# Cosine attention, FFT mixing and MLP on one core: identity-matmul transposes for the first two batches, three weight chunks in flight, five row buffers

## The chip, the cores and the metric

The kernel runs on one core of a Trainium2 chip. The core has a matrix engine (TensorE; PE in the profile, with PEld for the loading of its stationary operand), a vector engine (VectorE, DVE), a scalar engine (ScalarE, ACT), GpSimd (POOL), SyncE (SP), and 16 DMA engines that serve the queues of SP and POOL. SBUF is the on-chip memory of 128 partitions; PSUM has 8 banks of 512 f32 values per partition and takes what TensorE computes. The metric is the device time of one execution in microseconds, the median of several runs.

## What is computed

```python
q_n = q / (norm(q, axis=-1) + 1e-06)          # q, k, v: [8, 12, 448, 64]
k_n = k / (norm(k, axis=-1) + 1e-06)
attn = softmax(q_n @ k_n.T / tau)             # tau = 0.1
x = (attn @ v), heads side by side            # [8, 448, 768]
u = x + real(fft(fft(x, axis=1), axis=2))
un = (u - mean(u)) / sqrt(var(u) + 1e-06)     # over the 768
out = u + maximum(un @ w_ch1, 0) @ w_ch2      # 768 -> 3072 -> 768
```

## The kernel before

The eight batches run one after another through the same stages, and stages of neighbouring batches overlap. A planner in Python (class `Plan`) takes every operation with its possible engines, a modelled duration, a priority and the names that it reads and writes; `schedule()` builds one static list per engine from that, and `emit()` writes each list with semaphore waits. At run time each engine goes through its list in order: an instruction that waits holds everything behind it on its engine. PSUM is shared out as three pools of tiles: M has two tiles (one bank each; the outputs of the MLP matmuls), G two (two banks each; scores and FFT), V one (two banks; PV).

*Rows of Q and K.* A batch has seven row blocks: three of Q and three of K with 128 rows, and a tail block with the last 64 rows of each. `norm(b)` loads a block (SP), squares it (ScalarE, L584), sums each head (VectorE, L586), takes logarithm and exponential for the norm (ScalarE, `norms`, L463 and L465), and scales the rows to bf16 (VectorE, L592) into a buffer QH. Of QH's four rows of 768, two take scaled rows from batch 2 on and the other two serve as an f32 buffer for the squares; batch 1 uses all four for scaled rows. A DMA transpose on SP then writes QT (or KT): 64 channels of two heads on the partitions, tokens along the row. Batch 0 is handled by `first_norm`, in two groups of six heads: K and Q with the tail are scaled, and four DMA transposes (L545) write KT and QT. Copies into KTD place the 64 tail tokens of K for two heads on a block diagonal.

*Scores.* The FFT over tokens is folded: token s and token 448 - s are handled together. So the scores of two heads are computed in two halves of 225 columns, first tokens 0 to 224 read from QT, then token 0 followed by tokens 447 down to 224 read from QR, a copy of QT in reversed order (`qdup` and `qrev`; VectorE and ScalarE for batch 0, POOL at L627 after). QK is at L674, with the tail at L686 and L687. ScalarE takes the exponential (L655), PV follows (L702 for the tail of V in VZ, L705), then reciprocal, scaling, fold and the FFT matmuls (`fft`, L752 and L785).

*Normalized rows.* Each block of u is normalized by VectorE (L842) and transposed by DMA on SP (L846) into unT, inside the buffer UNT.

*MLP.* `ffn(b)` computes h = W1 x unT in 24 groups of six matmuls (L874), evacuated with relu by ScalarE or VectorE (L883, L884), and y = hT x W2 in groups of 24 (L895), added to u (L904) and stored. The MLP of batch 0 goes in two passes, first one block of rows (128 columns), then two (256 columns); the others have 384 or 512 columns. TensorE's list mixes the MLP of one batch with the attention of the next.

*Weights.* `weights` brings W1 and W2 in 12 chunks each, cast to bf16 by DMA from POOL's queue; each waits until the second last before it has landed. Loads of batch 2 on SP are gated on the tenth chunk of W2 (`self.w[21]`), loads of batch 1 on the scaled rows of batch 0 (`raw0`) and one transpose (`trs[3]`), the first loads of V on a transpose of batch 0.

## Time and profile before

| | us |
|---|---|
| median of 3 runs (677.9 to 682.45) | 677.96 |
| the profiled execution, whole | 682.08 |
| its span in the trace | 679.9 |
| TensorE busy | 594.6 (87%) |
| VectorE busy | 379.3 (56%) |
| ScalarE busy | 337.3 (50%) |
| GpSimd busy | 99.4 (15%) |

A busy time is the union of the instructions of one engine; the modelled ends of TensorE's matmuls overlap. "PEclk" is the TensorE clock that was granted, as a share of full speed. An idle time carries the releaser that the trace infers: what ended last before the instruction began. L12 is line 12 of the kernel. A line in the group view can hold several shapes ("+3 forms"), and then its mean is a mean over them.

### The profile page before, as it was taken

How to read it: one execution, taken by the hardware profiler on the slowest of the kernel's cores; microseconds unless marked ns; L12 is line 12 of the kernel's file. 1: busy time of each engine (PE TensorE's matmuls, PEld its weight loads, DVE VectorE, ACT ScalarE, POOL GpSimd, SP SyncE). 2: the span in 40 equal slices, each digit the busy share in tenths (PEclk: the TensorE clock that was granted, in tenths of full speed). 3: DMA queues.
4: the chain of work that ended last, by engine and by line, in shares of the span. 5: the costliest groups of instructions: out<-in, count | busy, mean ns of one | idle time of the engine just before them, and what ended most of it. 6: DMA issues, size and time to landing. Idle time of an engine off the chain costs nothing.

```text
span 679.9 us, 12298 instructions
## 1 busy us (share of the span) xinstructions
PE 594.6 (87%) x5040; PEld 372.0 (55%) x5040; DVE 379.3 (56%) x808; ACT 337.3 (50%) x608; POOL 99.4 (15%) x127
## 2 busy tenths in 40 slices
PE   0364578996999879998999999989999999999996
PEld 0143456763456546674556566755565667654463
DVE  5658723595575776559655964586758233810010
ACT  7686346622675138724674358534763256404300
POOL 2612242300100410021002110211020010000001
PEclk9988578997999989999999999999999999999998
DMA  8999999998734935095419561957157310210011
GB/s 179 125 181 144 139 176 132 168 125 180 109 60 80 138 90 108 20 131 137 93 37 118 107 156 34 113 92 163 25 67 72 78 48 1 44 50 24 0 47 48
DMA packets 210264, 65.29 MB, mean 96 GB/s; under 512 B 194080, under 2 KB 207904, under 8 KB 210208
## 3 DMA queue, kind: packets, MB, share of 16 engines
q1 hardware_dynamic: 152288, 41.70, 35.3%
q0 software_dynamic: 57920, 22.81, 27.0%
q8 instruction: 40, 0.66, 0.4%
q14 instruction: 16, 0.13, 0.1%
HBM read 51.90 MB, written 11.01 MB: 93 GB/s over the span
## 4 chain that ended last, share of the span: by engine, by line
PE 55%; DMA 4%; DVE 1%; issue 1%; POOL 1%; POOLq 0%; SPq 0%; DVEq 0%
PE PS L895 23%; PE PS L874 22%; PE PS L674 3%; DMA QT<-QH 3%; PE PS L705 3%; PE PS L752 1%; PE PS L702 1%; PE PS L785 1%; DVE QH L592 1%; POOL QR L627 1%; PE PS L687 0%; PE PS L686 0%; DMA UNT<-F 0%; POOLq L956 0%; DVE AC L734 0%
## 5 line engine op out<-in xcount | busy, mean ns | idle before, releaser
L874 PE MATMUL PS<-UNT,W1b 128*128 128x512 bf16 (+3 forms) x1296 | 245.6, 344 | 31.3 <-DMA UNT<-F 20.9
L895 PE MATMUL PS<-W2b,hT 128*128 128x384 bf16 x1344 | 226.6, 328 | 0.0
L874 PEld LDWEIGHTS PS<-UNT,W1b 128*128 128x128 bf16 x1296 | 122.4, 102 | 128.3 <-issue 30.9
L655 ACT ACTIVATE E<-PS 128x900 bf16<-128x900 f32 (+1 forms) x192 | 149.0, 825 | 87.0 <-PE PS L674 80.4
L895 PEld LDWEIGHTS PS<-W2b,hT 128*128 128x128 bf16 x1344 | 130.7, 98 | 86.3 <-issue 4.3
L883 ACT ACTIVATE hT<-PS 128x512 bf16<-128x512 f32 (+3 forms) x139 | 69.2, 498 | 100.9 <-PE PS L874 93.2
L904 DVE TENSOR_TENSOR OUTB<-PS,U 128x384 f32<-128x384 f32 x56 | 31.0, 554 | 107.4 <-PE PS L895 107.1
L884 DVE TENSOR_SCALAR hT<-PS 128x512 bf16<-128x512 f32 (+3 forms) x77 | 44.6, 579 | 64.3 <-PE PS L874 64.0
L674 PE MATMUL PS<-QT,KT 64*128 64x225 bf16 x288 | 35.4, 270 | 35.7 <-DVE QR L929 25.5
L592 DVE TENSOR_TENSOR QH<-STG,RN 128x768 bf16<-128x768 f32 x42 | 40.0, 953 | 27.6 <-DMA QT<-QH 15.6
L919 POOL DMA_INDIRECT out_dram<-OUTB,IDX x20 | 20.4, 1019 | 232.7 <-DVE OUTB L904 154.9
L705 PE MATMUL PS<-VB,E 128*128 128x65 bf16 x1152 | 53.5, 196 | 0.0
L635 POOL DMA_DIRECT2D VB<-in_v_dram x24 | 25.2, 1054 | 190.2 <-PE PS L705 185.3
L705 PEld LDWEIGHTS PS<-VB,E 128*128 128x128 bf16 x1152 | 50.1, 100 | 2.4
L702 PE MATMUL PS<-VZ,E 128*128 128x130 bf16 x192 | 43.1, 224 | 4.7 <-DMA VZ<-in_v_dram 2.9
L586 DVE TENSOR_REDUCE SS<-QH 128x12 f32<-128x768 f32 x42 | 39.4, 938 | 9.2 <-ACT QH L584 9.1
L674 PEld LDWEIGHTS PS<-QT,KT 64*128 64x128 bf16 x288 | 14.3, 94 | 52.9 <-DVE QR L929 25.5
L806 DVE TENSOR_TENSOR U<-SQT,X 128x384 bf16<-128x384 f32 (+3 forms) x80 | 42.3, 570 | 0.7
L584 ACT ACTIVATE QH<-STG 128x768 f32<-128x768 f32 x42 | 35.3, 840 | 10.1 <-DMA STG<-in_k_dram 9.4
L717 DVE RECIPROCAL RD<-PS 128x8 f32<-128x8 f32 x48 | 9.8, 204 | 52.5 <-PE PS L705 52.1
L674 PE MATMUL PS<-QR,KT 64*128 64x225 bf16 x288 | 35.0, 267 | 0.0
L719 DVE TENSOR_TENSOR X<-PS,RD 128x512 bf16<-128x512 f32 x48 | 33.1, 690 | 1.3
(92 smaller groups left out, 467.8 us busy)
## 6 DMA issues: line engine op xcount, KB each, us to landing
STG<-in_q_dram SPq DMA_DIRECT2D x18, 384.0 KB, 4.4
STG<-in_k_dram SPq DMA_DIRECT2D x18, 384.0 KB, 5.2
VB<-in_v_dram POOLq DMA_DIRECT2D x24, 192.0 KB, 7.2
W1b<-in_moe_w_ch_dram POOLq DMA_DIRECT2D x12, 384.0 KB, 6.2
W2b<-in_moe_w_ch_dram POOLq DMA_DIRECT2D x12, 384.0 KB, 6.0
out_dram<-OUTB SPq DMA_DIRECT2D x8, 384.0 KB, 2.5
hT<-in_q_dram SPq DMA_DIRECT2D x7, 192.0 KB, 5.6
hT<-in_k_dram SPq DMA_DIRECT2D x2, 576.0 KB, 5.0
```

The source lines that it names most:

```text
L584: P.add("act", lambda a, sq=sq, buf=buf: a.activation(sq, buf, ACTF.Square), t_act(DM), pr, f"sq{i}_{b}", reads=bn, writes=sqn, margin=1.0)
L586: P.add("dve", lambda v, i=i, sq=sq: v.tensor_reduce(SS[:, i, :], v3(sq), AX.X, AluOp.add), t_dve(DM), pr, f"ss{i}_{b}", reads=sqn, writes ...
L592: P.add("dve", lambda v, i=i, buf=buf, qh=qh: v.tensor_tensor(v3(qh), v3(buf), RN[:, i, :].unsqueeze(2).to_broadcast((128, H, DH)), AluOp. ...
L655: return a.activation(o, self.PS[:, bk:bk + nc_, 0:SQ2], ACTF.Exp, scale=1.0 / self.tau)
L674: i = pe.matmul(self.PS[:, bk + h, c0:c0 + NK], self.KT[r, jj, kt * 128:(kt + 1) * 128], Q[r, jj, 0:NK], start=True, stop=True)
L702: pe.matmul(o, st(6), self.VZ[:, j, :], start=True, stop=False, skip_group_check=True)
L705: r = pe.matmul(o[:, 65 * h:65 * h + 65], st(2 * kt + h), self.VB[:, kt, 2 * j + h, :], start=False, stop=(h == 1 and kt == 2), skip_group ...
L806: return v.tensor_tensor(U[o0:o0 + n, ut, cs].rearrange("p (i e) -> p i e", e=2), src, X[i0:i0 + n, x, cs].rearrange("p (i e) -> p i e", e ...
L874: r = pe.matmul(self.PS[:, bk, 0:n], self.W1b[:, j, ft * 128:(ft + 1) * 128], unT[:, j, cs], start=(j == 0), stop=(j == NJ - 1))
L883: return e.activation(self.hT[:, ft, cs], self.PS[:, bk, 0:n], ACTF.Relu)
L884: return e.tensor_relu(self.hT[:, ft, cs], self.PS[:, bk, 0:n])
L895: r = pe.matmul(self.PS[:, bk, 0:384], self.hT[:, ft, 128 * i:128 * i + 128], self.W2b[:, ft, 384 * c:384 * c + 384], start=(ft == 0), sto ...
```

## The change

1. The ScalarE program starts with an explicit load of the table set `natural_log_exp_and_others`.
2. VectorE builds ID, a 128 x 128 identity in bf16.
3. Batch 0: scaled K, Q and tail go through matmuls with ID as the moving operand into M tiles (three, five and three matmuls: `tk`, `tq`, `tt`), evacuated by ScalarE or VectorE into KT, QT and KTD, in place of four DMA transposes. The tail of Q and K is written to a place of its own. Column 448 of QT gets a second copy of token 0.
4. Batch 1: each scaled row block goes through two tiles of three identity matmuls (`tp`) with an evacuation each, in place of a DMA transpose; KTD is filled from the tail's matmuls.
5. Normalized rows of batch 0: six identity matmuls in the V tile (`tn`) and two evacuations, in place of a DMA transpose, three times.
6. QR is gone. QK reads QT backwards, columns 448 down to 224; from batch 1 on POOL copies the one column 448.
7. QH has five rows: four take scaled rows in every batch, the fifth takes squares in two halves of 384 from batch 2 on.
8. A weight chunk waits for the third last before it, not the second last.
9. Gates: the first three loads of batch 1 wait for the scaled rows of the first head group alone and are ordered after a load of batch 0 in place of a transpose; the first V loads wait for a load of batch 0 in place of a transpose.

```diff
+                if e == "act":
+                    nc.scalar.preload_act_table_set("natural_log_exp_and_others")
...
-        self.QH = T("QH", [128, 4, DM])
+        self.QH = T("QH", [128, 5, DM])
         self.QT = T("QT", [128, NJ, 512])
-        self.QR = T("QR", [128, NJ, NK])
...
+        P.add("dve", lambda v: v.tensor_scalar(self.ID[:], kcf[:, 0:128], self.rowf[:, 0:1], None, AluOp.is_equal), 0.3, -3, "id",
+              reads=["OUT1", "rowf"], writes=["ID"])
...
-        prev = [start, start]
+        prev = [start, start, start]
...
-            prev.append(P.add("pool", fn, 1.0, 9, nm, writes=[nm], dma=(nm, 16), after=[prev[-2]], serve=2.1))
-        self.w = prev[2:]
+            prev.append(P.add("pool", fn, 1.0, 9, nm, writes=[nm], dma=(nm, 16), after=[prev[-3]], serve=2.1))
+        self.w = prev[3:]
...
-                              ("Q", Q, [f"Sq{t}{g}" for t in range(3)], 18, uf[:, 0:1536], ["QL"]),
-                              ("T", R, [f"St{g}"], 6, uf[:, 0:1536], ["QLt"])], sq))
+                              ("Q", Q, [f"Sq{t}{g}" for t in range(3)], 18, uf[:, 0:1152], ["QL"]),
+                              ("T", R, [f"St{g}"], 6, uf[:, 1152:1536], ["QLt"])], sq))
...
-                if i == 1:
-                    continue
-                if i == 0:
-                    dst, src, rd, wr = self.KT[:, 3 * g:3 * g + 3], qh, qhn, [f"KT{t}_{g}" for t in range(3)]
-                else:
-                    dst, src, rd, wr = self.QT[:, 3 * g:3 * g + 3], qh, ["QL", "QLt"], [f"QT{t}_{g}" for t in range(4)]
-                dst = dst.rearrange("p j (t c) -> p (j t) c", c=128)
-                self.trs.append(P.add("sp", lambda sy, sem, dst=dst, src=src: sy.dma_start_transpose(dst, src).then_inc(sem, 16),
-                                      2.0, pr + g, f"tr{nm}{g}_0", reads=rd, writes=wr, dma=(f"t0{g}{i}", 16), serve=1.5 + 0.3 * i))
...
+            def evac(tile, dst, n, nm, wr):
+                def ev(e):
+                    i = self.PS[:, self.bank(tile), 0:n]
+                    return e.activation(dst, i, ACTF.Copy) if e is self.nc.scalar else e.tensor_copy(dst, i)
+                self.evac(ev, n, pr + g, nm, writes=wr, after=(tile.users[0],), tiles=(tile,))
+            for j in range(3):
+                jj = 3 * g + j
+                tile = Tile("M")
+
+                def fn(pe, tile=tile, j=j, kh=kh):
+                    for t in range(3):
+                        r = pe.matmul(self.PS[:, self.bank(tile), 128 * t:128 * t + 128], kh[:, 384 * j + 128 * t:384 * j + 128 * t + 128], ID[:],
+                                      start=True, stop=True)
+                    return r
+                P.add("pe", fn, 0.3, pr + g, f"tk{jj}_0", reads=kn + ["ID"], tiles=(tile,), acquire=tile)
+                evac(tile, self.KT[:, jj, :], 384, f"ek{jj}_0", [f"KT{t}_{jj}" for t in range(3)])
+                tile = Tile("M")
+
+                def fn(pe, tile=tile, j=j, qh=qh, th=th):
+                    o = self.PS[:, self.bank(tile), :]
+                    q3 = qh.rearrange("p (t c) -> p t c", t=3)[:, :, 128 * j:128 * j + 128]
+                    for t in range(3):
+                        pe.matmul(o[:, 128 * t:128 * t + 128], q3[:, t], ID[:], start=True, stop=True)
+                    pe.matmul(o[:, 384:448], th[:, 128 * j:128 * j + 128], ID[:, 0:64], start=True, stop=True)
+                    return pe.matmul(o[:, 448:449], q3[:, 0], ID[:, 0:1], start=True, stop=True)
+                P.add("pe", fn, 0.35, pr + g, f"tq{jj}_0", reads=qn + tn + ["ID"], tiles=(tile,), acquire=tile)
+                evac(tile, self.QT[:, jj, 0:449], 449, f"eq{jj}_0", [f"QT{t}_{jj}" for t in range(4)] + [f"QTd_{jj}"])
+            self.tails(pr + g, g, th, tn, 0)
...
+    def tails(self, pr, g, th, tn, b):
+
+        tile = Tile("M")
+
+        def fn(pe):
+            for j in range(3):
+                r = pe.matmul(self.PS[:, self.bank(tile), 64 * j:64 * j + 64], th[:, 128 * j:128 * j + 128], self.ID[:, 64:128],
+                              start=True, stop=True)
+            return r
+        self.P.add("pe", fn, 0.15, pr, f"tt{g}_{b}", reads=tn + ["ID"], tiles=(tile,), acquire=tile)
+        for x in range(2):
+            rows = slice(64 * x, 64 * x + 64)
+
+            def ev(e, rows=rows, x=x):
+                i = self.PS[rows, self.bank(tile), 0:192].rearrange("p (j c) -> p j c", j=3)
+                o = self.KTD[rows, 3 * g:3 * g + 3, 64 * x:64 * x + 64]
+                return e.activation(o, i, ACTF.Copy) if e is self.nc.scalar else e.tensor_copy(o, i)
+            self.evac(ev, 192, pr, f"et{g}_{b}", writes=[f"KTD{x}_{3 * g + y}" for y in range(3)], after=(tile.users[0],), tiles=(tile,))
...
-        order = [self.trs[3]] if b == 1 else []
+        order = [self.loads[9]] if b == 1 else []
...
-                after = self.raw0
+                after = self.raw0[0:3] if i < 3 else self.raw0
...
-                sqn, sq, nq = ["QH2", "QH3"], self.QH[:, 2:4, :].rearrange("p a b -> p (a b)").bitcast(F32), 2
-            P.add("act", lambda a, sq=sq, buf=buf: a.activation(sq, buf, ACTF.Square),
-                  t_act(DM), pr, f"sq{i}_{b}", reads=bn, writes=sqn, margin=1.0)
-            P.add("dve", lambda v, i=i, sq=sq: v.tensor_reduce(SS[:, i, :], v3(sq), AX.X, AluOp.add),
-                  t_dve(DM), pr, f"ss{i}_{b}", reads=sqn, writes=[f"SS{par}_{i}"])
-            self.norms(b, pr, 12 * i, 12 * i + 12, [f"SS{par}_{i}"], [f"RN{par}_{i}"])
-            r = self.qh_next % nq
+                sqn, sq, ns = ["QH4"], self.QH[:, 4, :].bitcast(F32), 2
+            w = DM // ns
+            for x in range(ns):
+                P.add("act", lambda a, sq=sq, src=buf[:, w * x:w * x + w]: a.activation(sq, src, ACTF.Square),
+                      t_act(w), pr, f"sq{i}_{b}", reads=bn, writes=sqn, margin=1.0)
+                P.add("dve", lambda v, o=SS[:, i, H // ns * x:H // ns * (x + 1)], sq=sq: v.tensor_reduce(
+                    o, sq.rearrange("p (h d) -> p h d", d=DH), AX.X, AluOp.add),
+                    t_dve(w), pr, f"ss{i}_{b}", reads=sqn, writes=[f"SS{par}_{i}" + "xy"[x]])
+            self.norms(b, pr, 12 * i, 12 * i + 12, [f"SS{par}_{i}" + x for x in "xy"[:ns]], [f"RN{par}_{i}"])
...
+            r = self.qh_next % 4
...
+            if b == 1:
+                if kind == "t":
+                    for g in range(2):
+                        self.tails(pr, g, qh[:, 384 * g:384 * g + 384], [f"QH{r}"], b)
+                for g in range(2):
+                    tile = Tile("M")
+                    n = 64 if kind == "t" else 128
+
+                    def fn(pe, tile=tile, g=g, qh=qh, n=n):
+                        for j in range(3):
+                            i = pe.matmul(self.PS[:, self.bank(tile), n * j:n * j + n], qh[:, 384 * g + 128 * j:384 * g + 128 * j + 128],
+                                          self.ID[:, 0:n], start=True, stop=True)
+                        return i
+                    P.add("pe", fn, 3 * t_mm(n), pr, f"tp{i}{g}_{b}", reads=[f"QH{r}", "ID"], tiles=(tile,), acquire=tile)
+                    dst = (self.KT if kind == "k" else self.QT)[:, 3 * g:3 * g + 3, 128 * t:128 * t + n]
+
+                    def ev(e, tile=tile, dst=dst, n=n):
+                        i = self.PS[:, self.bank(tile), 0:3 * n].rearrange("p (j c) -> p j c", j=3)
+                        return e.activation(dst, i, ACTF.Copy) if e is self.nc.scalar else e.tensor_copy(dst, i)
+                    self.evac(ev, 3 * n, pr, f"ep{i}{g}_{b}", writes=[("KT" if kind == "k" else "QT") + f"{t}_{3 * g + y}" for y in range(3)],
+                              after=(tile.users[0],), tiles=(tile,))
+                continue
...
-            for c0, c1, src, rd, nm, wr in ((0, 1, self.QT[:, :, 0:1], (0,), "qdup", "QD"),
-                                            (1, NK, self.QT[:, :, S - 1:NK - 2:-1], (1, 2, 3), "qrev", "QR")):
-                kw = dict(reads=[f"QT{t}_{y}" for y in g for t in rd], writes=[f"{wr}_{y}" for y in g])
-                if b == 0:
-                    self.copy(vw(self.QR[:, :, c0:c1]), vw(src), (c1 - c0) * n, 1, pr + g[0], f"{nm}{b}", **kw)
-                else:
-                    P.add("pool", lambda p, o=vw(self.QR[:, :, c0:c1]), i=vw(src): p.tensor_copy(o, i), t_pool((c1 - c0) * n),
-                          pr, f"{nm}{b}", **kw)
+                self.copy(self.KTD[rows, :, 64 * x:64 * x + 64], self.QT[rows, :, 448:512], 384, 4, pr, f"ktd{b}",
+                          reads=[f"QTd_{y}" for y in range(NJ)], writes=[f"KTD{x}_{y}" for y in range(NJ)])
+        if b:
+            P.add("pool", lambda p: p.tensor_copy(self.QT[:, :, 448:449], self.QT[:, :, 0:1]), 0.3, pr, f"qdup{b}",
+                  reads=[f"QT0_{y}" for y in range(NJ)], writes=[f"QTd_{y}" for y in range(NJ)])
...
-            gate = [self.trs[0 if t < 1 else 1]] if b == 0 else []
+            gate = [self.loads[8]] if b == 0 else []
...
-                        for c0, Q in ((0, self.QT), (NK, self.QR)):
+                        for c0, cols in ((0, slice(0, NK)), (NK, slice(S, NK - 2, -1))):
                             for h in (0, 1):
                                 r = slice(64 * h, 64 * h + 64)
                                 i = pe.matmul(self.PS[:, bk + h, c0:c0 + NK], self.KT[r, jj, kt * 128:(kt + 1) * 128],
-                                              Q[r, jj, 0:NK], start=True, stop=True)
+                                              self.QT[r, jj, cols], start=True, stop=True)
...
-                return pe.matmul(self.PS[:, bk, NK:SQ2], self.KTD[:, j, :], self.QR[:, j, :],
+                return pe.matmul(self.PS[:, bk, NK:SQ2], self.KTD[:, j, :], self.QT[:, j, S:NK - 2:-1],
...
+            if b == 0:
+                tile = Tile("V")
+
+                def fn(pe, tile=tile, nb_=nb_):
+                    for j in range(NJ):
+                        r = pe.matmul(self.PS[:, self.bank(tile) + j // 3, 128 * (j % 3):128 * (j % 3) + 128],
+                                      self.UN[:, nb_, 128 * j:128 * j + 128], self.ID[:], start=True, stop=True)
+                    return r
+                P.add("pe", fn, 0.4, lp, f"tn{ui}_{b}", reads=[f"UN{nb_}", "ID"], tiles=(tile,), acquire=tile)
+                for g in range(2):
+                    def ev(e, tile=tile, g=g, col=col):
+                        i = self.PS[:, self.bank(tile) + g, 0:384].rearrange("p (j c) -> p j c", j=3)
+                        o = self.unT[0][:, 3 * g:3 * g + 3, col:col + 128]
+                        return e.activation(o, i, ACTF.Copy) if e is self.nc.scalar else e.tensor_copy(o, i)
+                    self.evac(ev, 384, lp, f"eu{ui}{g}_{b}", writes=[f"unT0_{ui}" + "xy"[g]], after=(tile.users[0],), tiles=(tile,))
+                continue
```

TensorE's list at the start of the program, before (QT and QR are the two orders of Q, KTD the tail of K):

```order
L674 MATMUL PS<-QT,KT 128x225 x2
L674 MATMUL PS<-QR,KT 128x225 x2
L674 MATMUL PS<-QT,KT 128x225 x2
L674 MATMUL PS<-QR,KT 128x225 x2
L674 MATMUL PS<-QT,KT 128x225 x2
L674 MATMUL PS<-QR,KT 128x225 x2
L686 MATMUL PS<-QT,KTD 128x225
L687 MATMUL PS<-QR,KTD 128x225
```

and of the change, in the same place (QH holds the scaled K there, UNT the scaled Q and tail):

```order
L555 MATMUL PS<-ID,QH 128x128 x9
L566 MATMUL PS<-ID,UNT 128x128 x3
L567 MATMUL PS<-ID,UNT 128x64
L568 MATMUL PS<-ID,UNT 128x1
L566 MATMUL PS<-ID,UNT 128x128 x3
L567 MATMUL PS<-ID,UNT 128x64
L568 MATMUL PS<-ID,UNT 128x1
L566 MATMUL PS<-ID,UNT 128x128 x3
L567 MATMUL PS<-ID,UNT 128x64
L568 MATMUL PS<-ID,UNT 128x1
L737 MATMUL PS<-QT,KT 128x225 x4
L579 MATMUL PS<-ID,UNT 128x64 x3
```

Three K tiles and three Q tiles of the first head group now stand ahead of the first scores; the tail's tile stands behind the first four of them.

TensorE's list around the first MLP matmuls, where the FFT of batch 0 ends (L785, L848), before:

```order
L785 MATMUL PS<-CSd,Tt 128x192
L874 MATMUL PS<-UNT,W1b 128x128 x144
L874 MATMUL PS<-UNT,W1b 128x256 x30
L674 MATMUL PS<-QT,KT 128x225 x2
L674 MATMUL PS<-QR,KT 128x225 x2
```

and of the change (L652 are batch 1's Q and K, L914 the normalized rows F of batch 0, L957 the MLP's first product):

```order
L848 MATMUL PS<-CSd,Tt 128x192
L652 MATMUL PS<-ID,QH 128x64 x6
L914 MATMUL PS<-ID,F 128x128 x6
L957 MATMUL PS<-UNT,W1b 128x128 x30
L914 MATMUL PS<-ID,F 128x128 x12
L652 MATMUL PS<-ID,QH 128x128 x6
L957 MATMUL PS<-UNT,W1b 128x128 x18
L652 MATMUL PS<-ID,QH 128x128 x6
L957 MATMUL PS<-UNT,W1b 128x128 x18
L652 MATMUL PS<-ID,QH 128x128 x6
```

The pattern of the last rows goes on; 108 MLP matmuls of 128 columns stand ahead of batch 1's first scores, where 144 of 128 and 30 of 256 columns did.

ScalarE's list in the attention of batch 1 (L655 and L718 are the exponentials), before:

```order
L655 ACTIVATE E<-PS 128x900 x2
L762 ACTIVATE Tt<-PS 128x2x450
L655 ACTIVATE E<-PS 128x900
L883 ACTIVATE hT<-PS 128x256
L655 ACTIVATE E<-PS 128x450
L762 ACTIVATE Tt<-PS 128x2x450
L584 ACTIVATE QH<-STG 128x768
```

and of the change:

```order
L718 ACTIVATE E<-PS 128x900 x3
L718 ACTIVATE E<-PS 128x450
L966 ACTIVATE hT<-PS 128x256
L718 ACTIVATE E<-PS 128x900 x3
L630 ACTIVATE QH<-STG 128x384
L718 ACTIVATE E<-PS 128x450
L966 ACTIVATE hT<-PS 128x256
L718 ACTIVATE E<-PS 128x900 x3
```

The first square of a row of batch 2 (from STG) stood behind the last exponential of batch 1, beside the FFT evacuations of L762; now the first of its halves stands between the exponentials.

## Rows read from the trace of the kernel before

**Rows 1.** Windows by stage: start:end, length, busy us by engine, PEclk, DMA share, GB/s

```profile
25.50:62.20 36.70, 24.89 (x300) 16.34 (x300) 22.47 (x48) 29.43 (x41) 11.10 (x10) 0.91 1.22 170
62.20:73.60 11.40, 0.01 (x1) 0.04 (x2) 9.66 (x23) 2.41 (x7) 2.58 (x4) 0.63 1.18 126
73.60:99.00 25.40, 18.06 (x176) 15.54 (x178) 13.07 (x31) 10.49 (x35) 10.47 (x14) 0.70 1.54 162
...
130.20:163.80 33.60, 26.54 (x179) 16.72 (x177) 27.94 (x62) 10.43 (x28) 6.73 (x8) 0.95 1.06 151
163.80:600.00 436.20, 422.90 (x3602) 261.00 (x3603) 270.28 (x574) 228.73 (x413) 47.12 (x49) 0.98 0.54 87
```

**Rows 2.** Waits of PE, whole run: waiter and releaser: us, times, longest us

```profile
PE PS L674 <- DVE QR L929: 25.5, 1, 25.5
PE PS L874 <- DMA UNT<-F: 20.9, 3, 11.4
PE PS L874 <- ACT hT L883: 6.4, 4, 2.4
...
PE PS L674 <- POOL QR L627: 3.1, 2, 1.8
...
PE PS L702 <- DMA VZ<-in_v_dram: 2.9, 1, 2.9
PE PS L674 <- issue: 2.8, 2, 2.6
```

**Rows 3.** Timeline of the start: start us, us, instruction, [idle before, releaser]

```profile
12.43 1.28 ACT L463 ACT_TABLE_LOAD   x1
...
15.61 0.18 DVE L466 TENSOR_SCALAR SS<-SS 128x24 f32<-128x24 f32 x1 [2.17 <-ACT SS L465]
...
18.25 1.42 SPq L545 DMA_TRANSPOSE QT<-UNT  x1
...
25.02 0.40 DVE L929 COPY QR<-QT 128x672 bf16<-128x672 bf16 x1
```

**Rows 4.** Groups by form, from 160 us on: busy us, mean ns, idle before

```profile
L884 DVE TENSOR_SCALAR hT<-PS 128x384 bf16<-128x384 f32 x24 | 13.3, 555 | 16.0 <-PE PS L874 16.0
L883 ACT ACTIVATE hT<-PS 128x384 bf16<-128x384 f32 x48 | 23.5, 490 | 21.6 <-PE PS L874 21.4
```

**Rows 5.** Timeline, batch 0's last row transpose and first MLP matmul

```profile
67.02 11.17 SPq L846 DMA_TRANSPOSE UNT<-F  x3
...
73.59 3.36 PE L874 MATMUL PS<-UNT,W1b 128*128 128x128 bf16 x30 [11.44 <-DMA UNT<-F]
```

**Rows 6.** Timeline, batch 0's second MLP product to batch 1's first

```profile
135.65 0.96 PE L752 MATMUL PS<-CSs,F 128*128 128x225 bf16 x8 [1.42 <-DVE F L737]
...
140.43 17.71 PE L895 MATMUL PS<-W2b,hT 128*128 128x384 bf16 x108
...
158.65 0.47 DVE L842 TENSOR_SCALAR F<-U,MV,RS 128x768 bf16<-128x768 bf16 x1
...
163.78 18.83 PE L874 MATMUL PS<-UNT,W1b 128*128 128x512 bf16 x78 [5.64 <-DMA UNT<-F]
```

**Rows 7.** DMA queues, 20 to 31 us: packets, MB, share of the engines

```profile
q0 software_dynamic: 5456, 0.69, 99.4%
```

**Rows 8.** Timeline, the last rows of batch 1, from 87 to 99 us

```profile
87.31 0.96 DVE L592 TENSOR_TENSOR QH<-hT,RN 128x768 bf16<-128x768 f32 x1 [0.99 <-DMA QT<-QH]
...
97.42 1.38 POOL L627 COPY QR<-QT 128x1344 bf16<-128x1344 bf16 x1
...
98.95 0.27 PE L674 MATMUL PS<-QT,KT 64*128 64x225 bf16 x2
```

**Rows 9.** DMA, 46 to 57 us: rate in 40 slices, and the weights' queue

```profile
GB/s 0 0 0 13 73 73 97 151 192 188 188 194 184 183 184 190 201 195 199 196 123 35 71 45 32 104 181 188 192 201 194 199 147 125 162 171 190 195 199 190
...
q0 software_dynamic: 3050, 1.54, 111.3%
```

**Rows 10.** The page's groups: sums and squares of a row

```profile
L586 DVE TENSOR_REDUCE SS<-QH 128x12 f32<-128x768 f32 x42 | 39.4, 938 | 9.2 <-ACT QH L584 9.1
...
L584 ACT ACTIVATE QH<-STG 128x768 f32<-128x768 f32 x42 | 35.3, 840 | 10.1 <-DMA STG<-in_k_dram 9.4
```

57 lines of the change are left out of this document (29 added, 28 removed).

## The prediction

> **What bounds the kernel now.** I read the stages first. From 163.8 to 600 us TensorE is busy 422.9 of 436.2 us at clock 0.98 [rows 1]; there only TensorE's own work counts, and the change removes none of it. The idle time lies ahead of that. TensorE does nothing before the first scores at 25.5 us; it is busy 24.9 of 36.7 us in the attention of batch 0, not at all from 62.2 to 73.6, 18.1 of 25.4 us at clock 0.70 up to 99, and 26.5 of 33.6 us from 130 to 164 [rows 1, 5]. The waits of TensorE say for what [rows 2]: 25.5 us for the reversed copy QR of batch 0 at the start, 20.9 us in three waits for the DMA transposes of the normalized rows (UNT), 6.4 us for evacuations of hT, 2.9 us for the V tail of batch 1 (VZ), and 3.1 + 2.8 us, both at QK, where the QR copy on POOL was late (after the longest, 2.6 us, the copy had just ended). So what counts is how early the first scores, the first MLP matmul and the scores of batch 1 start; afterwards TensorE runs through.
>
> **1. First scores, 25.47 to about 19.0.** Before: after the scale of K, DVE waits 2.17 us for ScalarE, which loads two activation tables (from 12.43 on and again, 1.28 us each); Q and its tail are scaled until the transpose is issued at 18.25, and a reversed copy that ends at 25.42 releases QK [rows 3]. The new preload leaves one table set until the sines, so the four reloads of lines 463 and 465 go; the two late ones, 2.6 us, move the scaled Q and tail from 18.2 to 15.6. K's own scale does not move: its sums wait behind the reduction of Q. By the order, one evacuation of K stands ahead of Q's scale and two behind it, then the three Q tiles in turn on two banks. A 384-column evacuation takes 0.56 us on DVE and 0.49 on ScalarE [rows 4]; the Q tiles have 449 columns, I take 0.6. 15.6 + 0.55 + 2 x 0.55 = 17.3; two evacuations of Q free the banks for the third tile, 18.5; its five matmuls, 19.0. **Minus 6.5.** An identity matmul has no row here. Nearest: 30 matmuls of 128 columns in 3.36 us at clock 0.5, 0.112 each [rows 5]; at full clock 0.164/3 = 0.055, from 108 of 384 columns in 17.71 us [rows 6]. I take 0.112 here. The Trainium skill ("TensorE: Matmul & The Clock Gate", Part 4: PE-mode transpose) gives 275 ns for one such transpose in context, and "Perfetto Trace Analysis", Transposes, says that a logical transpose should use the transpose mode and not a standard matmul, as here. By the 275 ns taken one after another, an estimate, this step would gain some 2.5 us less; no run here shows it yet.
>
> **2. Attention of batch 0, 3 us given back.** ScalarE gets five evacuations (2.6 us), two for KTD and the Ln/Exp pairs of group 1 (together some 2) into a stretch where it was busy 29.4 of 36.7 us [rows 1]. I let 2.9 of 4.6 us show; bounds 0 and 4.6. PV of the first heads also waits for V. V's load is now gated on a Q load instead of a transpose, so it starts some 6 us earlier; it filled the engines over 11 us [rows 7] and now shares them with loads of batch 1. I take it to land near 27, 8 us behind the first QK, which is as far as before. The first normalized rows are then ready 3.6 us earlier, 63.4 instead of 67.0.
>
> **3. First MLP matmul, 73.59 to about 65.4.** From the issue at 67.02 to the matmul lie 6.6 us [rows 5]. Six identity matmuls (0.7 us), their latency, and two evacuations on ScalarE make 2.0. **Minus 8.2** so far.
>
> **4. Scores of batch 1, 98.95 to about 86.5.** DVE was busy 13.1 of 25.4 us here [rows 1]; it waited 0.99 us for a DMA transpose to free a row buffer, and the reversed copy ended at 98.80, with QK at 98.95 [rows 8]. Now each scaled row goes through two 3-matmul tiles and two evacuations. The scale of the last Q rows, which releases QK, ended at 88.3; 3.6 earlier, 1 us of buffer wait less, 1 us of added evacuations on DVE: 84.7, and 1.8 for matmuls and evacuations. **Minus 12.5.** What may hide or hold it: two banks (M) shared by the new tiles and h, both evacuated by the same two in-order queues.
>
> **5. To the MLP of batch 1, 163.78 to about 148.8.** Before, 64.8 us lie between, with waits of 2.9 (VZ), 1.42 (F) and 5.64 (UNT) [rows 2, 6]: 54.9 of work. Added: 36 matmuls of 128 and 30 of 256 columns that stood ahead of QK and now stand behind (2.0 + 3.3), new tiles 0.6, a cold start 1.5: 62.3. 86.5 + 62.3 = 148.8. VZ no longer waits, since V is loaded earlier. The DMA transposes of batch 1's rows stay; the last row was scaled 18.7 us after the last FFT matmul (140.43 to 159.1) and landed 4.7 later, 23.4 in all. All 144 y matmuls now stand behind that FFT: 144 x 0.164 = 23.6 us cover it. **Minus 15.0.** And the 78 matmuls after the old gap took 18.83 us where 78 x 0.219 = 17.1 would do, the half clock after idling: **minus 1.8**.
>
> **6. Later batches.** The reversed copy goes from POOL, and with it 3.1 + 2.6 us of waits [rows 2]: **minus 5.7**. The copy of one column that stays is short and waits for the first Q rows only; it also stands in POOL's list ahead of six W2 chunks, but those rows are ready long before. The third of the UNT waits, in batch 2 (20.9 - 11.4 - 5.6 = 3.9), I leave. Squares in two halves with one bf16 buffer add some 2 x 0.49 - 0.84 = 0.14 us on ScalarE and 2 x 0.56 - 0.94 = 0.18 on DVE for each of 42 rows [rows 4, 10], hidden while TensorE is the bound (DVE busy 270, ScalarE 229 of 436 us [rows 1]); without that cover 42 x 0.32 = 13 us. QK reads 336 operands backwards instead of a copy: at least no cost (DVE read the same columns backwards, 672 in 0.40 us [rows 3]), at most double, 336 x 0.096 = 32.3 us (225 of 384 columns of 0.164). I take none, as DVE's row shows no loss.
>
> **7. Weights.** With two in flight 1.54 MB, four chunks, came in 11 us, 2.8 us each, with dips between plateaus near 190 GB/s, that is 2.07 us a chunk [rows 9]. A third in flight fills the dips; bounds 2.07 and 2.8, I take 2.1. POOL reaches the first chunk near 37 (behind the table arguments), W1 is whole near 65, and W2's tenth chunk lands, with 9 us for V between, near 96. It must: batch 2's loads on SP are gated on it, and ScalarE's squares of batch 2 now stand inside the exponentials of batch 1.
>
> **Sum.** 15.0 + 1.8 + 5.7 = 22.5 from the profiled execution's 682.1 is 659.6. That execution is 4.1 over the median of 677.96; I keep this distance: 655.5, rounded 656.
>
> **Rivals.** (a) *The weights set the pace* (15%): at 2.8 us a chunk W2's tenth chunk lands near 112, batch 2's rows near 118, and ScalarE, which needs them at about 106, stands with the scores of batch 1 behind it: 8 to 12 lost, 664 to 668. For it: dips remain with other loads on the same engines; against: the plateau. (b) *The evacuations hold the banks* (12%): half of step 4 lost, 662. For it: 6.4 us of waits for hT already. (c) *Backward reads at half rate* (5%): place QK, price 32.3 less what ScalarE hides in batch 0, 30: 686, slower. It decides from 22 us on, that is from 0.065 us for each of the 336. The Trainium skill ("SBUF — State Buffer", Door 1) holds accesses within one 16-byte line free; that would make (c) nothing, but it is silent on direction. (d) *Better than worked out* (8%): nothing given back in step 2 (2.9), the UNT wait of batch 2 gone (3.9) and two more from the tail of step 4: 647. (e) *The change does not do what it says* (3%): the startup chain bound by loads, not tables and transposes, 672; against it the 2.17 us wait for ScalarE [rows 3].
>
> **Numbers.** The forecast, 648 to 663, has 57%. Leaving (c), (e) and the far ends outside, 646 to 669 holds 8 in 10. Faster by over 1% (below 671.2; about 1% is what a measurement of this kernel can tell from no change): 0.87. Same 0.07, slower 0.06, mostly (c).
>
> **What would show it.** First QK at 18 to 20.5; first MLP matmul at 64 to 67; first QK of batch 1 at 85 to 89; the last W1 chunk by 68; no gap ahead of batch 1's first 512-column matmul, at 147 to 151; no wait on POOL at QK. Backward QK matmuls beside forward ones in the groups show (c) at once; ScalarE idle on a load of STG near 105 shows (a). The prediction is wrong if TensorE's idle time before 164 us falls by less than 8 us.

## The result and the profile after

The changed kernel takes 651.2 us (median of 4 runs, 649.8 to 652.1) where the kernel before took 680.1 beside it: a ratio of 0.957, 95% interval 0.953 to 0.962. The forecast was 656, with a range of 646 to 669. The profiled execution took 651.6, with a span of 649.6 (679.9 before): 30.3 less where the sum had 22.5.

Medians here and below are over fast runs; left out as slow are one run of 670.4 us of the kernel with batch 1's rows by DMA, and seven (684.2 to 691.0) of the kernel before. The experiments ran in three groups on three chips, and beside them the kernel before had medians of 680.6, 683.1 and 676.0. So a difference of a few us between kernels of different groups, or between one of them and the change, is not told apart by the medians alone; where it matters, the text gives the ratio to the kernel before or goes by the timelines.

The windows by stage of the changed kernel (columns as in [rows 1]), cut at its first scores, first transposed row of batch 0, first scores of batch 1 and first 512-column matmul:

```profile
0.00:17.94 17.94, 2.83 (x24) 2.14 (x26) 13.41 (x27) 11.50 (x16) 8.62 (x29) 1.00 0.94 165
17.94:69.27 51.33, 30.39 (x346) 20.82 (x343) 32.65 (x67) 34.37 (x57) 18.53 (x20) 0.81 1.15 156
69.27:93.75 24.48, 15.82 (x156) 12.44 (x157) 20.16 (x46) 13.97 (x42) 11.76 (x16) 0.70 1.34 178
93.75:153.42 59.67, 59.42 (x632) 43.66 (x631) 44.75 (x108) 36.59 (x73) 6.39 (x8) 1.00 0.73 108
153.42:649.60 496.18, 490.21 (x4010) 298.97 (x4007) 272.96 (x609) 250.00 (x485) 44.06 (x49) 1.00 0.48 81
```

The same of the kernel before, its attention of batch 0 (first scores to the issue of the first row's transpose) and its last stage:

```profile
25.47:67.02 41.55, 24.91 (x300) 16.37 (x300) 27.32 (x60) 31.34 (x46) 12.16 (x11) 0.90 1.20 166
...
163.78:679.90 516.12, 496.76 (x4008) 300.63 (x4008) 276.95 (x585) 243.05 (x437) 51.96 (x54) 0.98 0.46 78
```

Two things are to be seen. The attention of batch 0 became 9.8 us longer (51.3 for 41.6), so that of 7.5 us won at the start nothing was left at its end. And from the first 512-column matmul to the end the time fell from 516.1 to 496.2, 19.9 us, at the same 4008 to 4010 matmuls: TensorE's idle time fell from 19.4 to 6.0 (what remains lies in the tail), and its busy time by 6.5, at a mean clock of 1.00 instead of 0.98.

| stage reached, us | before | forecast | after |
|---|---|---|---|
| first scores | 25.5 | 19.0 | 17.9 |
| first normalized row | 67.0 | 63.4 | 69.3 |
| first MLP matmul | 73.6 | 65.4 | 71.1 |
| first scores of batch 1 | 98.9 | 86.5 | 93.8 |
| first 512-column matmul | 163.8 | 148.8 | 153.4 |
| from there to the end | 516.1 | 508.6 | 496.2 |

TensorE's waits after (as in [rows 2]). Those for DMA transposes and for QR are gone, as is every gap behind 153.4 over 0.2 us; the longest that is left, behind the start, is 4.8 us for the first normalized row:

```profile
PE PS L555 <- DVE QH L534: 12.8, 1, 12.8
PE PS L914 <- DVE F L905: 5.7, 2, 4.8
PE PS L737 <- ACT E L718: 3.9, 6, 1.4
PE PS L765 <- issue: 3.5, 1, 3.5
...
PE PS L765 <- DVE X L782: 2.4, 2, 2.2
```

Where the 9.8 us went, the chain that ended last shows (start us, us, what), from the V load of batch 0 on:

```profile
16.34 10.67 DMA VB<-in_v_dram
27.02 1.42 issue
28.44 0.27 PE PS L765
...
31.70 0.63 DVE QT L547
32.33 0.99 DVE U L415 x3
...
34.65 4.19 POOL UNT L407
38.86 1.36 DVE UNT L409
...
40.37 0.70 DVE X L782
...
41.12 0.29 PE PS L765
```

The rows of V (VB) land at 27.0. Their tail VZ, which the first PV reads first, was issued in two parts at 18.6 and 19.3 and landed at 28.2:

```profile
L701 POOL DMA_DIRECT2D VZ<-in_v_dram x1: 664/664/664, 19.3 to 19.3; - x1
...
DMA to landing us min/median/max: 7.5/8.2/8.9
```

The first PV starts at 28.4, after 3.5 us in which TensorE stood. Behind that PV in TensorE's list are identity matmuls of the second head group; VectorE waits for their result (L547) with the arguments of the second FFT table behind it (L415); POOL needs those for its 5.4 us (L405, L407); and VectorE's last step on them (L409) stands ahead of the scaling X of the next heads, for which TensorE waits again. One late load went through three engines in order. It is not the whole of the 9.8 us. The first PV before:

```profile
32.80 0.29 PE L702 MATMUL PS<-VZ,E 128*128 128x130 bf16 x1
```

That is 7.3 us behind the first scores and 34.2 us ahead of the first normalized row. Now it is 10.5 and 40.8, so 3.2 us of the loss lie ahead of the first PV and 6.6 behind it.

### The profile page after: what moved, and what is told of

It is laid out like the page before. It is cut to its first block, busy times and chain, and to the rows that moved or that the text cites. A ratio compares the mean times of both kernels' runs of the same rounds, so it can differ in the third digit from the quotient of the medians.

```text
span 649.6 us, 12646 instructions
## 1 busy us (share of the span) xinstructions
PE 598.7 (92%) x5160; PEld 378.0 (58%) x5160; DVE 383.9 (59%) x853; ACT 346.4 (53%) x672; POOL 89.4 (14%) x120
## 3 DMA queue, kind: packets, MB, share of 16 engines
q0 software_dynamic: 57920, 22.81, 27.3%
## 4 chain that ended last, share of the span: by engine, by line
PE 88%; DVE 5%; DMA 3%; ACT 1%; POOL 1%; issue 1%; SPq 1%; POOLq 0%; DVEq 0%
PE PS L978 34%; PE PS L957 34%; PE PS L768 5%; PE PS L737 5%; PE PS L815 3%; PE PS L848 3%; PE PS L765 2%; DMA VB<-in_v_dram 2%; SPq L504 1%; DMA hT<-in_q_dram 1%; DVE U L869 1%; PE PS L749 1%; POOL UNT L407 1%; PE PS L750 1%; DVE ST L896 0%
## 5 line engine op out<-in xcount | busy, mean ns | idle before, releaser
L957 PE MATMUL PS<-UNT,W1b 128*128 128x512 bf16 (+3 forms) x1296 | 237.2, 336 | 2.4 <-ACT UNT L922 1.0
L957 PEld LDWEIGHTS PS<-UNT,W1b 128*128 128x128 bf16 x1296 | 119.8, 100 | 97.1 <-issue 4.5
L718 ACT ACTIVATE E<-PS 128x900 bf16<-128x900 f32 (+1 forms) x192 | 150.5, 824 | 24.4 <-PE PS L737 19.6
L966 ACT ACTIVATE hT<-PS 128x512 bf16<-128x512 f32 (+3 forms) x140 | 71.7, 513 | 95.7 <-PE PS L957 93.0
L967 DVE TENSOR_SCALAR hT<-PS 128x512 bf16<-128x512 f32 (+3 forms) x76 | 41.7, 548 | 36.1 <-PE PS L957 35.1
L632 DVE TENSOR_REDUCE SS<-QH 128x6 f32<-128x384 f32 x84 | 45.5, 542 | 11.0 <-ACT QH L630 10.5
L630 ACT ACTIVATE QH<-STG 128x384 f32<-128x384 f32 x84 | 43.6, 519 | 12.4 <-DVE SS L632 9.8
L737 PE MATMUL PS<-QT,KT 64*128 64x225 bf16 x576 | 44.6, 269 | 4.2 <-ACT E L718 3.9
L900 ACT ACTIVATE RS<-MV,cst 128x1 f32<-128x1 f32 x28 | 8.2, 294 | 66.6 <-DVE MV L898 66.5
L869 DVE TENSOR_TENSOR U<-SQT,X 128x384 bf16<-128x384 f32 (+3 forms) x80 | 40.8, 552 | 0.7
L737 PEld LDWEIGHTS PS<-QT,KT 64*128 64x128 bf16 x576 | 21.6, 96 | 20.5 <-ACT E L718 8.1
```

The costliest lines, as they stand in the source:

```text
L630: P.add("act", lambda a, sq=sq, src=buf[:, w * x:w * x + w]: a.activation(sq, src, ACTF.Square), t_act(w), pr, f"sq{i}_{b}", reads=bn, wri ...
L632: P.add("dve", lambda v, o=SS[:, i, H // ns * x:H // ns * (x + 1)], sq=sq: v.tensor_reduce(o, sq.rearrange("p (h d) -> p h d", d=DH), AX.X ...
L718: return a.activation(o, self.PS[:, bk:bk + nc_, 0:SQ2], ACTF.Exp, scale=1.0 / self.tau)
L737: i = pe.matmul(self.PS[:, bk + h, c0:c0 + NK], self.KT[r, jj, kt * 128:(kt + 1) * 128], self.QT[r, jj, cols], start=True, stop=True)
L869: return v.tensor_tensor(U[o0:o0 + n, ut, cs].rearrange("p (i e) -> p i e", e=2), src, X[i0:i0 + n, x, cs].rearrange("p (i e) -> p i e", e ...
L957: r = pe.matmul(self.PS[:, bk, 0:n], self.W1b[:, j, ft * 128:(ft + 1) * 128], unT[:, j, cs], start=(j == 0), stop=(j == NJ - 1))
```

## The experiments

Each edit is on the changed kernel unless it says otherwise; times are medians.

**V ahead of batch 1's loads.**

```diff
-                after = self.raw0[0:3] if i < 3 else self.raw0
+                after = (self.raw0[0:3] if i < 3 else self.raw0) + self.vl[:4]
```

> The changed kernel with one edit: the loads of batch 1 wait until V of batch 0 has landed (the lists of TensorE and of the other engines are otherwise the same). Theory A, V's late landing sets the attention of batch 0: in the changed kernel V lands at 27.0 us beside three loads of batch 1 and the first PV starts at 28.4 after 3.5 us of idle; VectorE's table arguments stand behind an evacuation that waits for that PV. Then V lands before 24.5, the first PV starts at 24.5 to 26, the first normalized row's transpose (69.3) comes 2.5 to 4 us earlier, at 65.3 to 66.8, and the first MLP matmul at 67 to 68.6 instead of 71.05. The end follows only as far as the rows of batch 1, now loaded some 5 us later, allow: 647 to 651. Rival B, the two PSUM banks and their evacuations set it: the first PV comes earlier, but the first normalized row stays within 1 us of 69.3.

644.8 us (five runs, 644.3 to 648.5; ratio 0.949, interval 0.942 to 0.955, where the change has 0.953 to 0.962): the lowest median here, with one more below beside it. The intervals touch; the timeline of TensorE shows the gain:

```profile
24.32 0.32 PE L765 MATMUL PS<-VZ,E 128*128 128x130 bf16 x1
...
64.81 0.82 PE L914 MATMUL PS<-ID,F 128*128 128x128 bf16 x6 [5.00 <-DVE F L905]
...
90.74 0.56 PE L737 MATMUL PS<-QT,KT 64*128 64x225 bf16 x8
```

The first PV comes 4.1 earlier and without a wait, the first normalized row 4.5, the scores of batch 1 3.0. Theory A holds, with the PV, the row and the time (647 to 651 expected) a little beyond what was expected; B falls. From the first PV to the row it still takes 40.5 us (40.8 in the change, 34.2 before): that part of the loss is not V's landing.

**The start alone, and the later parts alone.** The changed kernel with two row buffers and whole squares, two chunks, and a QR copy on POOL from batch 1 on (the three edits below in one); and the kernel before with backward reads, five row buffers and three chunks.

> The changed kernel with the late parts undone: two row buffers with whole squares, two weight chunks in flight, QR copied by POOL from batch 1 on. Theory C: the first scores stay at 18 and the first 512-column matmul of batch 1 comes at 153 to 157, but the waits for normalized rows and QR return, 10 us or more of idle behind it and half clock after each: from there to the end 510 to 516, time 664 to 672. Rival D: from there to the end 500 or less, time 653 to 658.

> The kernel before with only what concerns later batches: QR removed (backward reads), five row buffers, three weight chunks in flight; no preload, no identity matmuls. Theory C, the gain behind the first 512-column matmul of batch 1 (496.2 us from there to the end, 516.1 before) comes from these three: first 512-column matmul stays at 161 to 165, from there to the end 496 to 500, time 660 to 666. Rival D, it comes from the earlier start of batch 1, which leaves more MLP matmuls behind each FFT: only the QR waits go (5.7 us and some clock), from there to the end 508 to 512, time 670 to 676.

688.3 us (ratio 1.010, 1.001 to 1.020) and 680.4 (1.000, 0.997 to 1.004). Neither part is worth anything alone, and all four forecast times were missed. With the start alone the first 512-column matmul came at 162.2 (153 to 157 by theory C), and two of the waits for normalized rows were longer than any that batches 1 to 7 had before (5.6 at most; timeline of TensorE):

```profile
315.29 5.08 PE L960 MATMUL PS<-UNT,W1b 128*128 128x512 bf16 x13 [10.21 <-DMA UNT<-F]
...
468.88 8.76 PE L960 MATMUL PS<-UNT,W1b 128*128 128x512 bf16 x30 [8.57 <-DMA UNT<-F]
```

With the later parts alone its profile, the fastest of its ten runs, has 508.1 us from the first 512-column matmul on, as rival D had it, but the scores of batch 1 came at 106.0 (98.9 before), after 5.6 us in which TensorE stood. The rows of batch 1 go through DMA transposes there, with three weight chunks in flight, and from 75 us on these took 10.5 us to land (median; 9.8 to 12.7), where with two chunks before they took 8.7 (7.7 to 11.5). That the third chunk is the cause was not tried by itself. So I undid the parts one at a time.

**QR copied again.**

```diff
+            P.add("pool", lambda p: p.tensor_copy(self.QR[:], self.QT[:, :, S:NK - 2:-1]), t_pool(NK * NJ), pr, f"qrev{b}",
+                  reads=[f"QT{t}_{y}" for y in range(NJ) for t in range(4)] + [f"QTd_{y}" for y in range(NJ)], writes=["QR"])
```

> The changed kernel with one part undone: from batch 1 on POOL copies Q reversed into QR and QK reads the copy (batch 0 reads backwards as in the change). Theory C1, the QR copy is worth its waits: waits of QK for QR return, 3 to 6 us, time 654 to 658. Rival C2, with four row buffers the rows come earlier and the copy is hidden: waits under 1 us, time 650 to 653. If backward reads cost anything, the forward reads here show it: QK matmul mean below 259 ns behind 160 us.

654.0 us (651.1 to 655.6; ratio 0.961, 0.954 to 0.969), 2.8 more than the change, which the spread of the runs does not tell from nothing; at the edge of C1. One wait for QR over 1 us came back, where C1 had 3 to 6 us of them:

```profile
219.71 0.27 PE L740 MATMUL PS<-QT,KT 64*128 64x225 bf16 x2 [1.47 <-POOL QR L693]
```

The QK matmuls, all forward here, average 261 ns from QT and 257 from QR behind 160 us, beside 259 in the change: backward reads cost nothing that shows.

**Two row buffers.**

```diff
-                sqn, sq, ns = ["QH4"], self.QH[:, 4, :].bitcast(F32), 2
+                sqn, sq, ns = ["QH2", "QH3"], self.QH[:, 2:4, :].rearrange("p a b -> p (a b)").bitcast(F32), 1
-            r = self.qh_next % 4
+            r = self.qh_next % (4 if b == 1 else 2)
```

> The changed kernel with one part undone: from batch 2 on two row buffers and whole squares, as before (three chunks in flight, backward reads and all of the start as in the change). In TensorE's list the groups of six y matmuls (0.98 us each) between the last FFT matmul of a batch and its first MLP matmul are then 21, 22, 10, 27, 18, 28 for batches 1 to 6 (24, 19, 23, 32, 26, 40 in the change). Theory E, the row buffers set how much work covers the rows' way to unT, which takes some 20 us: a gap of 8 to 11 us ahead of batch 3's first MLP matmul, 2 or 3 ahead of batch 5's, half clock behind them; from the first 512-column matmul to the end 508 to 516, time 663 to 674. Rival F, it is the weight chunks that matter: no gap over 2 us, time 650 to 655.

668.8 us, 17.6 more (ratio 0.980, 0.974 to 0.986): theory E. From the first 512-column matmul to the end it takes 514.7 us instead of 496.2, so all of the loss lies there. The gaps came where the list has the least cover (timeline of TensorE, first MLP matmuls of batches 3 and 5):

```profile
305.44 4.90 PE L957 MATMUL PS<-UNT,W1b 128*128 128x512 bf16 x11 [10.80 <-DVE QH L639]
...
455.38 4.85 PE L957 MATMUL PS<-UNT,W1b 128*128 128x512 bf16 x16 [4.59 <-DMA UNT<-F]
```

The releaser named at 305, a scaling of Q or K rows that ended just then, writes nothing that this matmul reads; it reads the rows' transposes, the last of which was issued at 302.4 and landed near 305.

**Five buffers, with the order of two.** The question left was whether the buffers or the list cost the time.

```diff
             t = 0.0
+            t = max([0.0] + [d.end + SEM_LAT + op.margin for d in getattr(op, "late", ())])
...
+            late = self.trs[-2:-1] if b >= 2 else []
```

> The changed kernel with its five row buffers, but the planner is told that each scaled row from batch 2 on must wait until the row two before it is transposed, as two buffers would make it; no wait is added to the program, only the lists change. The y groups that cover the rows become 24, 18, 12, 26, 18, 26 for batches 1 to 6 (with two row buffers in truth 21, 22, 10, 27, 18, 28). Theory J, the order costs the time: gaps of 6 to 10 us ahead of batch 3's first MLP matmul and 2 to 5 ahead of batch 5's, time 662 to 670. Rival K, the buffers themselves do on the chip: no gap over 2 us, time 650 to 655.

671.7 us (ratio 0.989, 0.981 to 0.998), a little beyond theory J's 662 to 670, with its gaps:

```profile
306.86 6.42 PE L959 MATMUL PS<-UNT,W1b 128*128 128x512 bf16 x17 [9.15 <-DMA UNT<-F]
...
456.61 3.66 PE L959 MATMUL PS<-UNT,W1b 128*128 128x512 bf16 x11 [4.47 <-issue]
```

The chip had all five buffers; the order alone cost 20.5 us. What the order decides is how many groups of six y matmuls (0.98 us each, from 0.164 [rows 6]) stand between the last FFT matmul of a batch and the first MLP matmul that needs its rows, counted in TensorE's lists:

| y groups as cover | gap behind them, us |
|---|---|
| 10, 10 (start alone, two rows) | 10.2, 10.8 |
| 12, 14 (order of two, start alone) | 9.2, 8.6 |
| 15, 15, 16 (rows of batch 1 by DMA, before, before) | 7.1, 3.9, 3.0 |
| 18 (before, two rows, order of two twice, start alone) | 5.6, 4.6, 4.5, 1.9, 2.2 |
| 19, 19, 20, 20 (later parts alone, order of two, start alone, QR copied) | 2.6, 0.8, 1.0, 1.5 |
| 19 to 56 (all batches of the changed kernel) | none over 0.2 |

Where there is a gap, cover and gap make 18.5 to 23.3 us: that is what the rows take from the last FFT matmul through VectorE and the DMA to unT. Two batches do not fit. With the later parts alone batch 2 had 15 groups and no gap of its own, behind a wait of 3.1 us at QK; with two chunks in flight (below) batch 2 had 18 and no gap. In both, QK and PV matmuls of the next batch stand in the cover too (4.4 us in the second), and the count of y groups leaves those out.

**Two chunks in flight.**

```diff
-            prev.append(P.add("pool", fn, 1.0, 9, nm, writes=[nm], dma=(nm, 16), after=[prev[-3]], serve=2.1))
+            prev.append(P.add("pool", fn, 1.0, 9, nm, writes=[nm], dma=(nm, 16), after=[prev[-2]], serve=2.1))
```

> The changed kernel with one part undone: two weight chunks in flight. The y groups that cover the rows are 23, 18, 24, 32, 34, 46 for batches 1 to 6. Theory E: W1 and W2 land some 8 us later, yet no gap over 2 us comes behind the first 512-column matmul; time 650 to 656. Rival F: the scores of batch 2 or the first MLP matmuls of batch 0 wait for weights or for the gated loads, and the time is 660 or more.

655.5 us (654.2 to 658.9; ratio 0.960, 0.954 to 0.965), 4.3 more. The time is theory E's, but the loss comes by a wait for the gated loads as in rival F, in the attention of batch 1, which the prediction's rival (a) described: batch 2's loads wait for W2, ScalarE stands before the square of a row with the exponentials behind it, and TensorE with it (timeline):

```profile
111.46 0.60 SPq L621 DMA_DIRECT2D STG<-in_q_dram  x1
...
118.45 0.52 ACT L630 ACTIVATE QH<-STG 128x384 f32<-128x384 f32 x1 [7.15 <-DMA STG<-in_k_dram]
...
119.83 0.37 PE L749 MATMUL PS<-QT,KTD 128*128 128x225 bf16 x1 [6.52 <-ACT E L718]
```

**Batch 0's normalized rows by DMA, and batch 1's rows by DMA** (the condition `b == 0`, or `b == 1`, made false; in the second, KTD filled by copies as in the other batches).

> The changed kernel with one part undone: batch 0's normalized rows go through three DMA transposes instead of identity matmuls. The first MLP matmul comes 4 to 6 us later, at 75 to 77 instead of 71.05. Theory G, the rows of batch 1 on VectorE (squares, sums, scale, evacuation) set the first scores of batch 1: those stay within 1.5 us of 93.75, and the time within 2 us of 651.2. Rival H, the MLP matmuls ahead of them in TensorE's list set them: scores at 97 to 99, time 654.5 to 657.

> The changed kernel with one part undone: the rows of batch 1 go through seven DMA transposes, KTD through copies. The list puts 30 MLP groups ahead of batch 1's first scores (18 in the change) and leaves 15 y groups ahead of batch 1's first 512-column matmul (24). Theory G: scores of batch 1 at 96 to 99, a gap of 3 to 6 us ahead of the first 512-column matmul, time 656 to 662. Rival I: the transposes are hidden and the time stays within 2 us of 651.2.

650.6 us, nothing lost, and 661.9 (659.6, 661.9 and 669.0; ratio 0.968, 0.961 to 0.975), 10.7 lost, with a wide spread. The first waits 12.9 us for its transposes, and the scores of batch 1 come only 1.6 later all the same (theory G, just beyond its bound, and the time within it). The second pays at those scores, which its profile (of the run of 669.0) has at 107.6 where theory G had 96 to 99, and again at the first 512-column matmul. Its median is at the upper end of theory G's 656 to 662; rival I falls. Rows from the timelines, first of the one, then of the other:

```profile
77.31 2.96 PE L957 MATMUL PS<-UNT,W1b 128*128 128x128 bf16 x26 [12.90 <-DMA UNT<-F]
...
95.36 0.56 PE L737 MATMUL PS<-QT,KT 64*128 64x225 bf16 x8
```

```profile
107.63 0.94 PE L737 MATMUL PS<-QT,KT 64*128 64x225 bf16 x8 [7.00 <-DMA QT<-QH]
...
168.77 1.49 PE L957 MATMUL PS<-UNT,W1b 128*128 128x512 bf16 x3 [7.14 <-DVE SS L471]
```

At 168.77 too what the matmul reads is the last of the rows' transposes, which was issued at 164.9 and took 3.9 us to land. The transposes of batch 1's Q and K rows took 14.8 us (median; 11.5 to 17.1) to land in this run, with three weight chunks in flight, where the kernel before had 8.7. So part of what the identity matmuls are worth here is a price that the third chunk may have raised.

**No preload** (its two lines taken out).

> The changed kernel with one part undone: no explicit table load at the start (TensorE's list is the same). The first scores come 2 to 3 us later, at 20 to 21, since the table reloads stand ahead of Q's scale again. Theory A, V's landing at 27 sets what follows: the first PV stays within 1 us of 28.4 and the time within 1.5 us of 651.2. Rival N, the head start passes through: the first PV 2 us later, time 653 to 655.

651.2 us, nothing lost: theory A. The first scores come 4.3 later, more than expected, since four table loads of 1.28 us are back and the two early ones delay K too (its scaling starts at 13.3 instead of 11.3); the first PV is 0.6 later:

```profile
22.26 0.56 PE L735 MATMUL PS<-QT,KT 64*128 64x225 bf16 x4
...
29.01 0.32 PE L763 MATMUL PS<-VZ,E 128*128 128x130 bf16 x1
```

**Beyond the change.** With V ahead: the table's arguments ahead of the second head group's evacuations on VectorE; and, on top, evacuations of batch 0's and 1's rows and of the first MLP pass on ScalarE alone.

```diff
+            od = self.table_args([self.scl]) if g == 1 else []
...
+                self.evac(ev, n, pr + g, nm, writes=wr, after=(tile.users[0],), tiles=(tile,), order=od if nm[:2] == "eq" else [])
```

```diff
+        if name[:2] in ("ep", "eu") or (name[:4] == "relu" and name[-2:] == "_0" and n == 128):
+            self.P.add("act", fn, t_act(n), prio, name, **kw)
```

> V ahead of batch 1's loads, as in the run with that edit (644.8), and the arguments of the second FFT table stand on VectorE ahead of the evacuations of the second head group. Theory A2: POOL's part of the arguments, 5.4 us, starts 2 to 4 us earlier, X no longer waits behind VectorE's last step of the arguments (1.1 us of idle on TensorE goes), the first normalized row comes 1 to 2 us earlier than 64.8, time 642 to 644. Rival B2: the later chain over VectorE swallows it, time 644 to 646.

> The same, and the evacuations of batch 1's rows, of batch 0's normalized rows and of its first MLP pass go to ScalarE alone, which was busy 13.5 of 24 us between 67 and 91 where VectorE was busy 19.1. Theory L, VectorE sets the rows of batch 1: their first scores come 2 to 4 us earlier than 90.7, time 640 to 643. Rival M: ScalarE, in its own order, becomes as late, scores within 1 us of 90, time 642 to 646.

645.5 and 649.4 us. The first has its first normalized row at 62.7, 2.1 ahead of the run with V alone, the scores of batch 1 at 88.1 and the first 512-column matmul at 148.2, 2.0 ahead; but its median, in the range of B2, is not below the 644.8 that the other had on another chip. The two can't be told apart here. The second, beside the first on the same chip, has its scores at 88.3 and its first 512-column matmul at 151.0, 2.8 behind, at a mean clock of 0.95 between them (1.00 without the edit). Theory L falls, since the scores come no earlier, and the time is beyond rival M's too.

## Why the forecast held, step by step

The time fell into the range in part by luck. Two errors had opposite signs: the start gave 10.4 us up to the first 512-column matmul where 15.0 were forecast, and what follows gave 19.9 where 7.5 were. Of the miss that was left, 8.0 us between the profiled executions (651.6 where the sum gave 659.6), the median hides 3.7: the forecast kept the 4.1 us by which the execution profiled before lay above its median, and after the change it was 0.4.

Of the signs that the prediction named, the missing gap ahead of batch 1's first 512-column matmul, the missing waits on POOL at QK and TensorE's idle time ahead of 164 us (66.0 before, 45.0 after) came out. The first scores (17.9) were a little ahead of 18 to 20.5; the first MLP matmul, batch 1's first scores, its first 512-column matmul and the last chunk of W1 (landed near 71) were all later than named.

- *Step 1* was right in size (17.9 for 19.0) and without worth: without the preload the scores come 4.3 later and the end does not move. At the scores the other 3.2 us of 7.5 are what the identity matmuls and the backward reads bring together.
- *Step 2* failed. V was forecast near 27, and VB landed at 27.0, VZ at 28.2; wrong was "8 us behind the first QK, which is as far as before". Before, VZ landed at 32.1 (issued at 24.9, 7.2 us), 6.6 behind the first QK; now it is 10.3. TensorE stood for V, and the wait went on through lists in order to POOL's table arguments. "I let 2.9 of 4.6 us show" became 9.8. With V first the median is 6.4 us lower, and the first normalized row comes 4.5 earlier; the other 5.3 of the 9.8 lie behind the first PV and their cause stays open (VectorE's busy time in the stage rose from 27.3 to 32.7).
- *Step 3*: from the scaled row to the MLP matmul it took 1.8 us (69.2 to 71.1), 2.0 forecast. Its saving is not worth anything to the end: by DMA the first MLP matmul waits 12.9 us and the time stays. The rows of batch 1, not the MLP matmuls, set its scores. VectorE is busy 20.2 of 24.5 us between the first normalized row and those scores, but that it is what holds them is not shown: with the evacuations on ScalarE they came no earlier.
- *Step 4*: from the first MLP matmul to the scores of batch 1 22.7 us, 21.1 forecast. Of the 7.3 us by which the scores came later than forecast, 5.7 are the late start of this stage. Its identity matmuls are worth 10.7 us against DMA transposes with three chunks in flight.
- *Step 5*: no gap ahead of the first 512-column matmul, as forecast, and 59.7 us from the scores for 62.3. The 1.5 us for a cold start in that sum has no row, and none of it showed: the clock was 1.00 in this stretch.
- *Step 6* had the largest mistake. The row buffers were costed as a small loss hidden by TensorE, with nothing gained; taken back from the changed kernel they cost 17.6 us. The reason, more y matmuls behind each FFT, is the one that step 5 used for batch 1 and did not carry to batches 2 and 3, whose waits (3.9 "I leave", and 3.0 put down to VectorE) went. These 6.9 us, and the busy time behind the first 512-column matmul, which fell by 6.5 with the clock where half clock was counted once (1.8), make 11.6 of the 12.4 us that the forecast lacked there. Batch 3's wait goes with the later parts alone (24 groups of cover instead of 16); batch 2 then still has 15 groups, so its 19 in the change need the rest of it too. For QR 5.7 us were forecast, and waits of that size went; taken back, it cost 2.8, not clear of the spread.
- *Step 7*: loads of batch 2 started at 97.2 (the tenth W2 chunk forecast near 96). With two chunks they start at 111.5 (112 worked out for rival (a)), and that costs 4.3 by the medians, less than its 8 to 12.

Of the rivals (c) falls: behind 160 us the QK matmuls, half of them backward, average 259 ns:

```profile
L737 PE MATMUL PS<-QT,KT 64*128 64x225 bf16 x432 | 30.4, 259 | 0.2 <-issue 0.2
```

Before, all of them forward, those from QT took 261 and those from QR 256:

```profile
L674 PE MATMUL PS<-QT,KT 64*128 64x225 bf16 x216 | 25.1, 261 | 6.0 <-POOL QR L627 3.1 <-issue 2.8
L674 PE MATMUL PS<-QR,KT 64*128 64x225 bf16 x216 | 24.6, 256 | 0.0
```

Rival (d) named one term that did come, the UNT wait of batch 2. Of rival (b) little shows: from the first MLP matmul to the scores of batch 1, the stage that it would make 6 us longer took 1.6 more than forecast, though TensorE waits some 4.3 us there for evacuations by ScalarE. Rival (e) falls with the first scores at 17.9.

The single parts don't add up: undone one by one they cost 17.6, 10.7, 4.3, 2.8, 0 and 0 us, but the start without the later parts is no faster than before. What stays open is why the list of two buffers is worse with the new start (10 groups of cover in batch 3) than before (16). The change also raises the planned time of a row's DMA transpose from 1.0 to 1.75 us (`serve` in `norm`), which its description does not name. The lists are built from such times, so this may have a part in it and in the 19.9 us; it was not tried alone.

## What to carry to other kernels

Where a list is fixed ahead, ask of each buffer not only who waits for it on the chip, but what the planner puts ahead of what because of it: here the order alone cost as much as taking the buffers away. Count, at each stage's start, how much independent work stands between the producer and its consumer, and compare that with the time the rows take. And a start made earlier is worth only what the next arrival allows: look which load lands last before moving the work ahead of it.
